# An attention and two-layer expert kernel on one core: side steps and the products with v placed from a table of slots

## The chip, the cores and the metric

The kernel runs on one core of a Trainium2 chip. TensorE (PE) multiplies matrices, VectorE (DVE) and ScalarE (ACT) work on elements, GpSimd (POOL) does further elementwise work, and SyncE (SP) issues the transfers. Every engine follows its own list of instructions in a fixed order and waits on semaphores for the others. The metric is device time in microseconds (us) of one execution. The kernel before takes 518.95 us, the median of three runs (518.83 to 519.52).

## The reference

Three layers follow each other. Only the first is touched by the change.

```python
q_assign = argmax(q_n . c_n)            # nearest of 16 centroids, per query; k_assign likewise, per key
mask   = q_assign[..., :, None] == k_assign[..., None, :]
scores = where(mask, (q @ k.T) / 8, -1e9)
x = softmax(scores) @ v                 # 2 batches x 8 heads, 768 tokens, 64 wide
x = moe(x)                              # x @ w_in, a rational function P(h) / Q(h), @ w_out
out = moe2(x)                           # soft routing by phi to 8 experts with w1, w2
```

All of it is float32. The weights `w_in` and `w_out` reach the chip as 64-bit numbers and have to be turned into float32 on it ("decoding").

## The kernel before, in words

**Units and slots.** Attention handles two heads at a time: 8 pairs, p = 0 to 7. A pair has 12 units, each 128 queries of one head by all 768 keys, so there are 96 units. The main loop runs over n, and one turn of it is called a slot (slot n in what follows). In slot n, TensorE first turns the 128 x 768 softmax weights of unit n (six transpositions, line 359, tile sT). Then it computes the scores of unit n + 2 (four products, lines 335 and 336, tile s). VectorE takes the scores of unit n + 2 out of PSUM, scaled and with their row minimum (line 344, e). ScalarE takes the exponential of unit n + 1 (line 348) and copies the turned weights of unit n (line 365, eT). There is one PSUM tile for s and one for sT, so the scores of the next unit cannot start until VectorE has read the last ones, and the next transpositions wait for ScalarE's copy.

**Products with v.** Six units (one half of a pair) form a group g, and six blocks of products with v belong to it (line 372, av, one block is two heads). The string AV says how many blocks TensorE does in each slot; they come after the scores.

**Side steps.** Three kinds of work are laid between these. (1) `prep(p)` makes the operands of a pair two pairs ahead: scores against the centroids (line 216), their scaled copy and transposition, the one-hot cluster of each token (`best`, `first`: lines 231 to 246), its transposition and mask (`ohT`, `masks`), and the split of k and q into two rounded parts on GpSimd (`ksplit`, `qsplit`); transfers (`ksplit(1)`, `ksplit(2)`, `qspreads`, `mspread`: 4 + 2 + 6 + 8 per pair) then spread these into the operand tiles k1, k2, q1, q2. (2) `norm(g)` and `a2_x(g)` divide by the softmax sum and split the result. (3) 32 decoding steps, one every 2.65 slots (list DEC): a load, two bit operations, an exponent on ScalarE, mantissa and sign on VectorE (lines 492, 493, 499, 503), a product on GpSimd (line 508), a store; for `w_out` also a product with phi (`tr`, `tcopy`, `mm`, `keep_`, every fourth time `fin`, `total`).

**What sets the order.** The order on every engine is written by this loop. A dictionary `plan` holds, for each slot and each kind of phase, the side steps of that slot in the order in which they were added. VectorE's steps of slot n stand before its line 344 for unit n + 2; GpSimd's and SyncE's are issued at the slot's head; TensorE's transpositions (phase P) stand between scores and products with v, its other products (phase T) behind them. Before, a step's slot follows from offsets in the return lists of `prep`, `norm`, `wphi_steps` (and PREP1 for pair 1). SyncE issues in program order and rotates over eight completion semaphores: each transfer waits until the one eight places before it has landed.

After attention the second stage (lines 747 to 780, 48 units) follows, then the last layer.

Of the kernel before, what the change touches and what calls it, by code (L numbers as in the profile page):

```python
# [8 lines left out]
F32 = mybir.dt.float32  # L9
F32R = mybir.dt.float32r  # L10
# [4 lines left out]
ALU = mybir.AluOpType  # L15
# [37 lines left out]
def tile_kernel(ctx, tc, qT, kT, v, cenT, cenP, consts, constsb, ab, w_in, w_out, phi, w1, w2, out, dbg=None):  # L53
# [59 lines left out]

    LEAD = 2
    PREP1 = (0, 0, 1, 1, 2, 3, 3, 4, 5, 6, 2, 3, 5, 7)
# [23 lines left out]
    def first_pair(r, o, f):  # L139
# [51 lines left out]
        def back(nxt):  # L191
# [3 lines left out]
        rest = [(0, "G", lambda: f["qsplit"](1)),  # L195
                (1, "S", lambda: f["qspreads"](slice(HS, S))),
                (1, "D", lambda: q_rows(0, 1)),
                (2, "D", lambda: q_rows(1, 1))]
        return front, back, rest

    def prep(p):
# [81 lines left out]
        def qsplit(c, done=None):  # L283
# [17 lines left out]
        if p == 0:  # L301
            return first_pair(r, o, locals())
        b = 1 if p == 2 else 0
        return [
            (1 + b, "T", scores),
            (2 + b, "A", scaled),
            (3 + b, "P", scT),
            (4 + b, "D0", lambda: best(0)),
            (4 + b, "D0", lambda: best(1)),
            (5 + b, "D0", lambda: first(0)),  # L310
            (8, "G", lambda: ksplit(0)),
            (6 + b, "D0", lambda: first(1)),
            (7 + b, "D0", lambda: first(2)),
            (7 + b, "P", ohT),
            (8 + b, "A", masks),
            (11, "G", lambda: qsplit(0)),
            (12, "G", lambda: qsplit(1)),
            (9, "S", lambda: ksplit(1)),
            (10, "S", lambda: ksplit(2)),
            (10 + b, "S", mspread),  # L320
            (13, "S", qspreads),
        ]
# [52 lines left out]
    def norm(g):  # L375
# [24 lines left out]
        at = (0, 1, 2, 4, 5) if g < 2 * NP - 1 else (0, 1, 1, 2, 3)  # L400
        return list(zip(at, ("G0", "D0", "G0", "P", "A"), (total, over, wide, rows, keep_)))

    def a2_x(g):
# [21 lines left out]
        return [(0, "D0", scale), (1, "G", split)]  # L425
# [54 lines left out]
    def decode_steps(i, src, dst, after=None):  # L480
# [38 lines left out]
        def store():  # L519
            SP.dma_start(dst, hold["w" if after else "w2"])  # L520

        return [(-4, "L", dma), (0, "D1", bits), (1, "A", expo), (1, "D1", mant), (2, "D1", sign),
                (3, "G0", value)] + ([(4, "S", store)] + after(hold) if after else [(4, "G", parts), (5, "S", store)])
# [4 lines left out]
    def wphi_steps(f):  # L528

        def steps(hold):  # L530
# [26 lines left out]
            def total():  # L557
# [3 lines left out]
            return [(4, "P", tr), (5, "A", tcopy), (6, "T", mm), (7, "D1", keep_)] + \  # L561
                ([(7, "P", fin), (8, "D1", total)] if f % 4 == 3 else [])
# [19 lines left out]
    def w_load(n):  # L582
        for a in range(2):
# [32 lines left out]
    steps = prep(1)  # L616
    early = [steps.pop(0)[2] for _ in range(3)]
# [3 lines left out]
    for slot, (_, eng, fn) in zip(PREP1, steps):  # L621
        plan.setdefault(slot, {}).setdefault(eng, []).append(fn)
    pend = None
    for n in range(-LEAD, NSL + 6):
# [10 lines left out]
        if k == 4 and n > 0 and p + 2 < NP:  # L635
            add(n, prep(p + 2))
# [18 lines left out]
        run(n, ("S", "D0", "D", "D1", "D2", "G0", "G"))  # L655
# [668 lines left out]
```

## Time and profile before

| | before |
|---|---|
| median of 3 runs | 518.95 us (518.83 to 519.52) |
| profiled execution | 518.78 us, its span 517.0 us |
| first and last start of a transposition of attention (line 359) | 20.4 and 271.4 us |
| TensorE busy in the span | 501.1 us (97%) |
| VectorE, ScalarE, GpSimd busy | 404.5, 362.7, 274.3 us |

A busy share of TensorE near 100% does not say that it works at its peak: matmuls are pipelined and their ends are modelled, so a wait can hide inside an instruction that seems to run. What a slot costs is read from the distance between the first transpositions of neighbouring units.

### The profile page before, as it was taken

The numbers are of one execution on the slowest core, as the hardware profiler recorded it, in microseconds if no ns is written. First come the engines' busy times: TensorE is split into PE (matmuls) and PEld (weight loads), VectorE is DVE, ScalarE is ACT, GpSimd is POOL, SyncE is SP. The second block draws the span as 40 slices with busy tenths as digits, with TensorE's granted clock in tenths as the row PEclk, the third lists the DMA queues.
The fourth block names the chain that finished last, engine by engine and source line by source line (L and its number), as shares of the span: only waits on it lengthen the run. The fifth ranks groups of instructions, "written<-read, shape, count | busy, mean of one in ns | idle before, by whom it ended". The sixth has DMA issues, their size and how long they took to land.

```text
span 517.0 us, 9835 instructions
## 1 busy us (share of the span) xinstructions
PE 501.1 (97%) x3446; PEld 336.0 (65%) x3446; DVE 404.5 (78%) x746; ACT 362.7 (70%) x646; POOL 274.3 (53%) x316
## 2 busy tenths in 40 slices
PE   8899999999999999999999999999999999999994
PEld 3556666666666666666666877777777768764362
DVE  5698899798998988988642999999799996985022
ACT  2587778888778888778772888879588786861111
POOL 4253876549686496765423856555365544551000
PEclk9999999999999999999999999999999999999999
DMA  7998989787996869873402767766466765789997
GB/s 218 249 227 223 315 244 301 223 248 218 261 298 173 285 200 287 249 216 129 160 5 61 261 226 263 278 223 234 181 228 235 266 231 178 289 325 403 422 418 307
DMA packets 44944, 126.18 MB, mean 244 GB/s; under 512 B 7136, under 2 KB 9696, under 8 KB 40288
## 3 DMA queue, kind: packets, MB, share of 16 engines
q1 hardware_dynamic: 44752, 125.31, 73.9%
q8 instruction: 27, 0.44, 0.4%
q10 hardware_dynamic: 144, 0.26, 0.1%
q14 instruction: 21, 0.17, 0.1%
HBM read 89.56 MB, written 15.73 MB: 204 GB/s over the span
## 4 chain that ended last, share of the span: by engine, by line
PE 67%; DMA 13%; DVE 9%; ACT 5%; SPq 2%; issue 1%; POOL 1%; ACTq 0%; DVEq 0%
PE h L747 9%; PE av L372 9%; PE sT L359 9%; PE h L750 9%; PE h L748 9%; DMA wt<-w 7%; PE s L335 5%; PE s L336 4%; DVE e L344 4%; PE gt L794 4%; DMA raw<-w_out 3%; ACT e L348 2%; PE l L806 2%; SPq L299 2%; ACT eT L365 2%; DMA w_in<-w 1%
## 5 line engine op out<-in xcount | busy, mean ns | idle before, releaser
L348 ACT ACTIVATE e<-e,nv 128x768 f32<-128x768 f32 x96 | 90.0, 937 | 46.7 <-DVE e L344 42.4
L344 DVE TENSOR_SCALAR_CACHE_REDUCE e<-s 128x768 f32<-128x768 f32 x96 | 91.5, 954 | 32.9 <-PE s L336 25.6
L359 PEld LDWEIGHTS sT<-cst,e 128*128 128x128 f32 x576 | 61.3, 140 | 46.6 <-ACT eT L365 24.5
L359 PE MATMUL sT<-cst,e 128*128 128x128 f32 x576 | 83.7, 281 | 2.5 <-ACT eT L365 2.0
L747 PE MATMUL h<-xh,w 128*128 128x512 f32 x192 | 80.6, 420 | 0.0
L365 ACT COPY eT<-sT 128x768 f32<-128x768 f32 x96 | 75.4, 785 | 6.0 <-PE sT L359 5.6
L372 PE MATMUL av<-eT,vt 128*64 128x384 f32 x384 | 77.2, 504 | 0.0
L764 POOL TENSOR_SCALAR q<-u,babs 128x512 f32<-128x512 f32 x47 | 36.3, 771 | 73.9 <-ACT u L762 73.9
L508 POOL TENSOR_TENSOR w<-mh,ex 128x516 f32<-128x516 f32 x32 | 41.2, 1287 | 64.5 <-DVE ex L503 44.9
L748 PE MATMUL h<-xl,w 128*128 128x512 f32 x192 | 75.3, 392 | 0.0
L335 PE MATMUL s<-k,q 128*128 128x384 f32 x192 | 73.5, 383 | 1.7 <-DVE e L344 1.5
L336 PE MATMUL s<-k,q 80*128 80x384 f32 x192 | 65.1, 339 | 1.1 <-DMA k<-kb 0.6
L766 POOL TENSOR_TENSOR q<-q,u 128x512 f32<-128x512 f32 x47 | 60.9, 1297 | 3.8
L750 PE MATMUL h<-xh,w 128*128 128x512 f32 x192 | 52.9, 396 | 0.0
L762 ACT ACTIVATE u<-h 128x512 f32<-128x512 f32 x47 | 27.9, 594 | 27.6 <-PE h L750 24.0
L747 PEld LDWEIGHTS h<-xh,w 128*128 128x128 f32 x192 | 36.1, 188 | 16.2 <-DVE r L780 4.2
L765 DVE TENSOR_TENSOR p<-p,h 128x512 f32<-128x512 f32 x47 | 32.1, 682 | 15.0 <-ACT p L763 14.9
L750 PEld LDWEIGHTS h<-xh,w 128*128 128x128 f32 x192 | 36.0, 188 | 8.6
L335 PEld LDWEIGHTS s<-k,q 128*128 128x128 f32 x192 | 36.4, 189 | 6.7 <-DVE e L344 5.9
L748 PEld LDWEIGHTS h<-xl,w 128*128 128x128 f32 x192 | 36.2, 189 | 6.7 <-issue 0.5
L772 ACT ACTIVATE r<-q,epsc 128x512 f32<-128x512 f32 x47 | 32.8, 698 | 9.2 <-POOL q L766 7.4
L336 PEld LDWEIGHTS s<-k,q 80*128 80x128 f32 x192 | 36.6, 190 | 1.8 <-issue 1.1
(198 smaller groups left out, 930.2 us busy)
## 6 DMA issues: line engine op xcount, KB each, us to landing
wt<-w SPq DMA_DIRECT2D x32, 1024.0 KB, 7.1
w<-w_in SPq DMA_DIRECT2D x96, 256.0 KB, 3.2
raw<-w_in SPq DMA_DIRECT2D x16, 512.0 KB, 5.0
raw<-w_out SPq DMA_DIRECT2D x16, 512.0 KB, 5.7
w_in<-w SPq DMA_DIRECT2D x16, 512.0 KB, 4.9
k<-ka SPq DMA_DIRECT2D x32, 192.0 KB, 5.1
q<-qh SPq DMA_DIRECT2D x28, 192.0 KB, 5.3
w_out<-w SPq DMA_DIRECT2D x16, 256.0 KB, 4.7
```

Of the source, the lines that this page charges most:

```text
L335: PE.matmul(ps[:, c, 0:HS], o["q1"][:, it], o["k1"][:, w], start=True, stop=False)
L336: PE.matmul(ps[:, c, 0:HS], o["q2"][0:80, it], o["k2"][0:80, w], start=False, stop=True)
L344: DVE.tensor_scalar(e, s1s.pop(u)[:, :, 0:HS], -(D ** -0.5), None, ALU.mult, ALU.min, accum_out=nvs[g][:, rest:rest + 1])
L348: ACT.activation(es[u], es[u], AF.Exp, scale=-1.0, bias=nvs[g][:, rest:rest + 1], accum_out=sums[g][:, rest:rest + 1])
L359: PE.transpose(ps[:, j // 3, j % 3 * 128:(j % 3 + 1) * 128], e[:, j, :], ident)
L365: ACT.copy(dst, eTp.pop(u)[:, :, 0:HS].rearrange("p c (j t) -> p c j t", j=3))
L372: PE.matmul(av[g][64 * h:64 * h + 64, 0:HS], vs[g // 2][:, h, j, :], eTs[g][:, h, j, :], start=(j == 0), stop=(j == 5))
L508: POOL.tensor_tensor(w.rearrange("p (r n) -> p r n", r=3), hold["mh"].bitcast(F32), hold["ex"].bitcast(F32), ALU.mult)
L747: PE.matmul(h, wh[:, c, :], xh[t][:, c, :], start=(c == 0), stop=False)
L748: PE.matmul(h, wh[:, c, :], xl[t][:, c, :], start=False, stop=False)
L750: PE.matmul(h, wl[:, c, :], xh[t][:, c, :], start=False, stop=(c == NCC - 1))
L766: POOL.tensor_tensor(q, q, u, ALU.mult)
```

## The change

The offsets and PREP1 go. A table SLOT gives the slot of every side step by number: for the steps of a pair one entry per pair (indexed from the end), for those of a group one per group, for phi one per decoded block. The steps of decoding itself keep their slots. `best`, `first`, `ksplit` and `qsplit` are cut so that each single instruction has a slot of its own. Inside a slot, each engine's steps are sorted by a fixed list (RANK) instead of by the order in which they were added. AV is another string.

```diff
-    PREP1 = (0, 0, 1, 1, 2, 3, 3, 4, 5, 6, 2, 3, 5, 7)
+    SLOT = {
...
+        "best0": (0, 10, 21, 34, 43, 53, 71),
+        "best1": (0, 11, 22, 35, 45, 53, 71),
...
+        "mspread": (5, 18, 30, 43, 54, 64, 79),
...
+        "kspread1": (5, 16, 31, 39, 49, 62, 77),
+        "qspread": (3, 14, 29, 37, 55, 65, 78),
...
+    }
+    RANK = {n: i for i, n in enumerate(
+        "x over best0 best1 f0 f1 f2 keep total mant sign bits".split()
+        + "sum wide ka kb0 kb1 qh0 ql0 qh1 ql1 value parts split".split()
+        + "scaled r tcopy expo masks".split() + "rows scT ohT tr fin".split() + "mm scores".split())}
...
+    def step(slot, name, fn):
+        return slot, (PHASE[name], RANK.get(name, 0)), fn
...
+        def round_k():
+            tile_(t_p, "ka", [128, S], F32R)
+            tile_(t_p, "kb", [128, S], F32R)
+            POOL.tensor_scalar(hold["ka"], r["k"], 1.0, 1.0, ALU.mult, ALU.mult)
+
+        def low_k(c):
+            w = slice(c * HS, (c + 1) * HS)
+            POOL.tensor_tensor(hold["kb"][:, w], r["k"][:, w], hold["ka"][:, w].bitcast(F32), ALU.subtract)
...
-            (4 + b, "D0", lambda: best(0)),
-            (4 + b, "D0", lambda: best(1)),
-            (5 + b, "D0", lambda: first(0)),
-            (8, "G", lambda: ksplit(0)),
...
+        early = [] if p > 1 else EARLY
+        return [steps[n] for n in early], [step(SLOT[n][p - NP], n, fn) for n, fn in steps.items() if n not in early]
...
-        at = (0, 1, 2, 4, 5) if g < 2 * NP - 1 else (0, 1, 1, 2, 3)
-        return list(zip(at, ("G0", "D0", "G0", "P", "A"), (total, over, wide, rows, keep_)))
+        return [step(6 * g + 6, "sum", total)] + [step(SLOT[n][g], n, fn) for n, fn in
+                                                  zip(("over", "wide", "rows", "r"), (over, wide, rows, keep_))]
...
-          "201111111201102021120201102201"
-          "111102111021121101012201112101"
-          "020211120201301101112101101112"]
+          "110211210201101130131010112101"
+          "201012021021120102102210221010"
+          "102030211020301110211011111030"]
...
-            for fn in plan.get(slot, {}).pop(eng, []):
+            for _, _, fn in sorted(plan.get(slot, {}).pop(eng, []), key=lambda x: x[:2]):
                 fn()
...
-        if k == 4 and n > 0 and p + 2 < NP:
-            add(n, prep(p + 2))
+        if k == (2 if p else 4) and n > 0 and p + 2 < NP:
+            add(0, prep(p + 2)[1])
...
-        run(n, ("S", "D0", "D", "D1", "D2", "G0", "G"))
+        run(n, ("S", "D", "G"))
```

**VectorE, slots 69 and 70.** Each piece begins with line 344 for unit 70 and ends with that for unit 72 (its line is 391 in the changed file). L242 and L244 are two steps of `first`, L550 and L558 `keep_` and `total` of phi, L499 the mantissa, L503 the sign, L492 and L493 the bit operations. Before:

```order
L344 TENSOR_SCALAR e,nv<-s_2628 128x768
L242 TENSOR_TENSOR eq<-eq,cb 128x384
L550 COPY wph<-mf 128x128
L499 SCALAR_TENSOR_TENSOR mh<-raw_141,mh 128x3x172
L344 TENSOR_SCALAR e,nv<-s_2658 128x768
L244 TENSOR_REDUCE mr<-eq 128x24
L558 TENSOR_REDUCE wphi_79<-mf 128x128
L503 SCALAR_TENSOR_TENSOR ex<-raw_141,ex 128x3x172
L492 TENSOR_SCALAR ex<-raw_142 128x3x172
L493 TENSOR_SCALAR mh<-raw_142 128x3x172
L344 TENSOR_SCALAR e,nv<-s_2691 128x768
```

Now:

```order
L391 TENSOR_SCALAR e,nv<-s_2621 128x768
L546 SCALAR_TENSOR_TENSOR mh<-raw_141,mh 128x3x172
L391 TENSOR_SCALAR e,nv<-s_2650 128x768
L550 SCALAR_TENSOR_TENSOR ex<-raw_141,ex 128x3x172
L539 TENSOR_SCALAR ex<-raw_142 128x3x172
L540 TENSOR_SCALAR mh<-raw_142 128x3x172
L391 TENSOR_SCALAR e,nv<-s_2683 128x768
```

Two steps of `first`, `keep_` and `total` have left these two slots; the decoding steps have stayed.

**SyncE, the operands of pair 1.** The names in k_1 and q_1 are the second set of operand tiles; the number behind is the head. w_in_138 is the store of the first decoded block (512 KB). Before, the last transfers ahead of pair 1's first unit are:

```order
L264 DMA k_1_1_132<-nh 16x384
L520 DMA w_in_138<-w_502 128x1024
L299 DMA q_1_0_125<-qh 64x768
L299 DMA q_1_0_125<-ql 64x768
L299 DMA q_1_0_126<-qh 64x768
L299 DMA q_1_1_129<-qh 64x768
L299 DMA q_1_1_129<-ql 64x768
L299 DMA q_1_1_130<-qh 64x768
L486 DMA raw_141<-w_in 128x1024
```

Now:

```order
L311 DMA k_1_1_132<-nh 16x384
L332 DMA k_1_0_127<-ka 64x768 x2
L332 DMA k_1_1_131<-ka 64x768 x2
L335 DMA k_1_0_128<-kb 64x768
L335 DMA k_1_1_132<-kb 64x768
L567 DMA w_in_138<-w_515 128x1024
L533 DMA raw_141<-w_in 128x1024
```

The six q transfers have moved ahead of the masks, the six k transfers (two rows stand for two each) are the last, and the store comes behind them instead of in front.

**SyncE, the operands of pair 7.** Masks are the transfers out of nh; each pair has eight. raw loads a block to decode, w_in_138 and w_out_139 are stores of decoded ones. Before, the last transfers of pair 7 were the q parts, with the masks ahead of them and three transfers of decoding between:

```order
L264 DMA q_1_1_130<-nh 16x384
L264 DMA k_1_1_132<-nh 16x384
L520 DMA w_in_138<-w_2825 128x1024
L486 DMA raw_140<-w_in 128x1024
L520 DMA w_out_139<-w 128x512
L299 DMA q_1_0_125<-qh 64x768
L299 DMA q_1_0_125<-ql 64x768
L299 DMA q_1_0_126<-qh 64x768
L299 DMA q_1_1_129<-qh 64x768
L299 DMA q_1_1_129<-ql 64x768
L299 DMA q_1_1_130<-qh 64x768
```

Now the masks are the last, directly behind the q parts, of which the last three stand first here:

```order
L359 DMA q_1_1_129<-qh 64x768
L359 DMA q_1_1_129<-ql 64x768
L359 DMA q_1_1_130<-qh 64x768
L311 DMA q_1_0_126<-nh 16x384
L311 DMA k_1_0_128<-nh 16x384
L311 DMA q_1_0_126<-nh 16x384
L311 DMA k_1_0_128<-nh 16x384
L311 DMA q_1_1_130<-nh 16x384
L311 DMA k_1_1_132<-nh 16x384
L311 DMA q_1_1_130<-nh 16x384
L311 DMA k_1_1_132<-nh 16x384
L533 DMA raw_141<-w_out 128x1024
```

The masks have moved behind the q parts, and the three transfers of decoding that stood between have moved ahead of the whole batch of 20 transfers of the pair.

## Rows read from the trace of the kernel before

**Rows 1.** The page: the span; an engine, busy us (share), instructions.
```profile
span 517.0 us, 9835 instructions
...
PE 501.1 (97%) x3446; PEld 336.0 (65%) x3446; DVE 404.5 (78%) x746; ACT 362.7 (70%) x646; POOL 274.3 (53%) x316
```

**Rows 2.** Stages: start:end, us, engines' busy us (instructions), clock, DMA share, GB/s.
```profile
20.40:34.50 14.10, 13.26 (x77) 8.53 (x78) 13.31 (x25) 11.37 (x21) 3.61 (x5) 1.00 1.05 260
34.50:68.81 34.31, 32.99 (x221) 20.67 (x221) 30.07 (x54) 26.52 (x47) 24.12 (x26) 1.00 0.84 239
68.81:148.92 80.11, 79.02 (x550) 52.84 (x546) 71.44 (x138) 65.85 (x118) 54.47 (x66) 1.00 0.87 260
148.92:244.57 95.65, 94.56 (x639) 62.85 (x635) 84.06 (x156) 77.77 (x139) 65.24 (x76) 1.00 0.76 227
244.57:270.82 26.25, 26.06 (x178) 17.30 (x176) 15.04 (x35) 20.96 (x38) 9.20 (x15) 1.00 0.24 81
```

**Rows 3.** TensorE's timeline, units 60 to 64: start us, length us, instruction.
```profile
181.19 0.87 PE L359 MATMUL sT<-cst,e 128*128 128x128 f32 x6
...
183.49 0.87 PE L359 MATMUL sT<-cst,e 128*128 128x128 f32 x6
...
186.24 0.87 PE L359 MATMUL sT<-cst,e 128*128 128x128 f32 x6
...
189.18 0.87 PE L359 MATMUL sT<-cst,e 128*128 128x128 f32 x6
...
191.84 0.88 PE L359 MATMUL sT<-cst,e 128*128 128x128 f32 x6
```

**Rows 4.** VectorE's groups, 18:270 us: count, busy us, mean ns, idle before.
```profile
L344 DVE TENSOR_SCALAR_CACHE_REDUCE e<-s 128x768 f32<-128x768 f32 x96 | 91.5, 954 | 32.9 <-PE s L336 25.6 <-ACT e L348 4.0 <-ACT eT L365 2.6
L499 DVE SCALAR_TENSOR_TENSOR mh<-raw,mh 128x516 f32<-128x516 uint32 x32 | 31.6, 989 | 0.0
L503 DVE SCALAR_TENSOR_TENSOR ex<-raw,ex 128x516 int32<-128x516 int32 x32 | 28.3, 885 | 2.2 <-ACT ex L496 2.1
...
L492 DVE TENSOR_SCALAR ex<-raw 128x516 int32<-128x516 int32 x32 | 21.7, 677 | 0.0
```

**Rows 5.** Line 499 alone: count, shortest/median/longest ns, first and last start.
```profile
L499 DVE SCALAR_TENSOR_TENSOR mh<-raw,mh x32: 678/800/1777, 27.9 to 247.8; 128x516 f32<-128x516 uint32 x32
```

**Rows 6.** The timeline round slots 71 and 72, VectorE and TensorE.
```profile
211.89 1.50 DVE L499 SCALAR_TENSOR_TENSOR mh<-raw,mh 128x516 f32<-128x516 uint32 x1
...
213.11 0.87 PE L359 MATMUL sT<-cst,e 128*128 128x128 f32 x6
213.30 0.95 DVE L344 TENSOR_SCALAR_CACHE_REDUCE e<-s 128x768 f32<-128x768 f32 x1
...
214.31 0.44 PE L335 MATMUL s<-k,q 128*128 128x384 f32 x1 [0.33 <-DVE e L344]
```

**Rows 7.** TensorE in slot 10, the scores of unit 12.
```profile
46.80 0.41 PE L335 MATMUL s<-k,q 128*128 128x384 f32 x1 [0.29 <-DVE e L344]
47.70 0.42 PE L336 MATMUL s<-k,q 80*128 80x384 f32 x1 [0.48 <-DMA q<-ql]
```

**Rows 8.** SyncE's timeline: start us, length us, issues.
```profile
40.25 0.53 SPq L520 DMA_DIRECT2D w_in<-w  x1
...
55.23 2.85 SPq L278 DMA_DIRECT2D k<-ka  x4
```

**Rows 9.** DMA issues, 18 to 245 us: count, KB each, median us to landing.
```profile
q<-qh SPq DMA_DIRECT2D x28, 192.0 KB, 5.3
```

**Rows 10.** The same for 96 to 104.5 us.
```profile
q<-qh SPq DMA_DIRECT2D x4, 192.0 KB, 7.8
```

**Rows 11.** The timeline where attention ends, TensorE and ScalarE.
```profile
270.82 0.87 PE L359 MATMUL sT<-cst,e 128*128 128x128 f32 x6 [0.17 <-ACT eT L365]
...
271.73 0.80 ACT L365 COPY eT<-sT 128x768 f32<-128x768 f32 x1 [0.96 <-PE sT L359]
...
273.07 0.50 PE L747 MATMUL h<-xh,w 128*128 128x512 f32 x1
```

More of the change, by code (lines that the diff above doesn't have):

```diff
@@ L112, in tile_kernel @@
     NBUF = 2
+    SLOT = {
+        "xs": (15, 20, 25, 33, 41, 44, 49, 55, 65, 68, 73, 81, 84, 94, 96, 100),
+        "scores": (5, 16, 27, 39, 50, 67),
+        "scaled": (6, 17, 30, 41, 51, 68),
+        "scT": (9, 19, 31, 42, 52, 69),
[5 rows of a table added]
+        "ohT": (1, 16, 24, 40, 50, 59, 77),
+        "masks": (4, 17, 27, 41, 51, 62, 78),
+        "mspread": (5, 18, 30, 43, 54, 64, 79),
[9 rows of a table added]
+        "qspread": (3, 14, 29, 37, 55, 65, 78),
+        "over": (8, 15, 19, 25, 34, 37, 43, 52, 55, 62, 67, 73, 79, 86, 91, 98),
+        "wide": (8, 15, 20, 27, 34, 37, 43, 52, 55, 63, 68, 73, 79, 86, 93, 98),
+        "rows": (8, 16, 20, 27, 34, 37, 45, 52, 55, 63, 69, 75, 79, 87, 93, 98),
+        "r": (9, 17, 22, 28, 35, 39, 46, 53, 56, 64, 70, 76, 81, 89, 94, 99),
+        "tr": (8, 14, 19, 23, 29, 37, 42, 45, 52, 59, 63, 65, 71, 77, 83, 87),
+        "tcopy": (9, 15, 22, 25, 31, 39, 44, 49, 55, 62, 64, 68, 72, 80, 86, 91),
+        "mm": (14, 18, 23, 29, 35, 40, 48, 50, 58, 63, 65, 71, 79, 83, 88, 92),
+        "k0": (16, 19, 26, 31, 38, 44, 49, 52, 61, 65, 68, 73, 82, 85, 90, 93),
+        "fin": (34, 55, 75, 95),
+        "tot": (37, 56, 77, 96),
+    }
[3 more added lines that the diff above has]
+        + "scaled r tcopy expo masks".split() + "rows scT ohT tr fin".split() + "mm scores".split())}
+    PHASE = {n: e for e, ns in dict(
+        D="x over best0 best1 f0 f1 f2 keep total mant sign bits q_rows",
+        G="sum wide ka kb0 kb1 qh0 ql0 qh1 ql1 value parts split", A="scaled r tcopy expo masks",
+        P="rows scT ohT tr fin", T="mm scores", S="store kspread0 kspread1 mspread qspread", L="load").items()
+        for n in ns.split()}
+    def step(slot, name, fn):
+        return slot, (PHASE[name], RANK.get(name, 0)), fn
     LEAD = 2
-    PREP1 = (0, 0, 1, 1, 2, 3, 3, 4, 5, 6, 2, 3, 5, 7)
+    EARLY = ("scores", "scaled", "scT")
     OPENW = 4
@@ L193, in back @@
             idle(3)
[L195 to L198, printed above, removed]
+        rest = [step(0, "qh1", lambda: f["qsplit"](1)),
+                step(1, "qspread", lambda: f["qspreads"](slice(HS, S))),
+                step(1, "q_rows", lambda: q_rows(0, 1)),
+                step(2, "q_rows", lambda: q_rows(1, 1))]
         return front, back, rest
@@ L423, in split @@
                 done += n
-        return [(0, "D0", scale), (1, "G", split)]
+        return [step(6 * g + 12 if g < 2 * NP - 1 else NSL + 4, "x", scale), step(SLOT["xs"][g], "split", split)]
     NH = H // 2
@@ L520, in store, with at @@
             SP.dma_start(dst, hold["w" if after else "w2"])
-        return [(-4, "L", dma), (0, "D1", bits), (1, "A", expo), (1, "D1", mant), (2, "D1", sign),
-                (3, "G0", value)] + ([(4, "S", store)] + after(hold) if after else [(4, "G", parts), (5, "S", store)])
+        def at(i):
+            steps = [step(max(i - 4, -LEAD), "load", dma), step(i, "bits", bits), step(i + 1, "expo", expo),
+                     step(i + 1, "mant", mant), step(i + 2, "sign", sign), step(i + 3, "value", value)]
+            if after:
+                return steps + [step(i + 4, "store", store)] + after(hold)
+            return steps + [step(i + 4, "parts", parts), step(i + 5, "store", store)]
+        return at
     wph = {}
@@ L615, in tile_kernel @@
     SP.dma_start(coef, ab)
-    steps = prep(1)
-    early = [steps.pop(0)[2] for _ in range(3)]
+    early, steps = prep(1)
     front(early)
@@ L620, in tile_kernel @@
     add(-LEAD + 1, rest)
-    for slot, (_, eng, fn) in zip(PREP1, steps):
-        plan.setdefault(slot, {}).setdefault(eng, []).append(fn)
+    add(0, steps)
     pend = None
```

58 lines of the change are left out of this document (25 added, 33 removed), and 11 rows, old and new, of the table SLOT.

## The prediction

> **What bounds the kernel now.** I read the page first. TensorE is busy for 97% of the 517.0 us, ScalarE and VectorE for far less [rows 1], so the kernel looks bound by TensorE alone, and a change that only moves other work could then give nothing. The page's busy time is no proof of that, so the second view is the table of stages. Its bounds are the first transpositions of units 0, 6, 18, 48, 84 and 95 [rows 2]. Attention fills 250.4 of the 517.0 us, and up to unit 84 VectorE is busy 88 to 94% of each stage [rows 2]. Two engines are nearly full there, and in a slot in which VectorE has more to do than TensorE, TensorE has to wait.
>
> The third view is TensorE's timeline, for the price of a slot. In slots 60 to 63 the first transpositions stand at 181.19, 183.49, 186.24, 189.18 and 191.84 [rows 3]. Slot 60 holds one block with v: 2.30 us. Slot 61 has four transpositions for phi besides: 2.75. Slot 62 holds two blocks: 2.95. Slot 63 has one block and the product with phi: 2.66. So a second block costs 0.65, turning for phi 0.45, its product 0.36. Priced in this way from slots without a wait, TensorE's own list is 13.1 us for slots 0 to 5, 31.7 for 6 to 17, 77.5 for 18 to 47 and 91.6 for 48 to 83, together 213.9. The stages took 14.1, 34.3, 80.1 and 95.65 [rows 2], together 224.2. TensorE loses 10.3 us there: 1.0, 2.6, 2.6 and 4.05.
>
> Where it loses them is seen round slot 72. The transpositions of unit 72 start at 213.11, and the scores should follow 0.61 later, at 213.72. They start at 214.31, released by VectorE's line 344, which only started at 213.30 behind a mantissa step [rows 6]. That is 0.59 us in one slot. One other loss is of another kind: in slot 10 the second score product starts at 47.70, 0.90 behind the first, and waits for the transfer of q [rows 7]; undisturbed it follows after 0.26 (an estimate from the neighbouring pairs of products), so 0.64 us are lost to the transfer. The other 9.6 us I put down to VectorE.
>
> **VectorE's list.** Priced by mean durations [rows 4] less the 0.08 or so by which an instruction's record overlaps the next (the mantissa at 211.89 ends at 213.39, the next starts at 213.30 [rows 6]): line 344 with its wait 0.97, mantissa 0.91, sign 0.80, each bit operation 0.60, the smaller steps between 0.10 and 0.62. Take slot 70. Before, VectorE has 0.97 + 0.47 (`first`) + 0.59 (`total`) + 0.80 + 1.20 = 4.03 us, and TensorE 2.30 + 0.34 = 2.64 (one block and the transpositions of `rows`). Excess: 1.39. Now VectorE has 0.97 + 0.80 + 1.20 = 2.97, and TensorE three blocks, 3.60. Excess: none. Summed in this way over slots 0 to 83, VectorE's list is longer than TensorE's in 34 slots before, by 2.0, 3.6, 4.4 and 6.9 us in the four stages, 17.0 in all. The losses to VectorE, without the 0.64, are 1.0, 2.0, 2.6 and 4.05. The ratio is 0.50, 0.55, 0.59 and 0.59: about 0.57 of an excess turns into time, and the rest is taken up by the slack of a slot or so between the engines. That the ratio holds in four stages is the best evidence that this is the mechanism.
>
> **The change part by part.**
> The work is the same: the same instructions of the same shapes on every engine, none added, none taken away. What changes is what stands beside what.
> - TensorE's list over slots 0 to 83 becomes 213.0 (14.0, 30.2, 76.7 and 92.1): a few switches between kinds of products less. Term: -0.9 us.
> - VectorE's excess falls to 9.6 us in 23 slots (2.0, 0.8, 3.8 and 2.9). At the ratios of the stages the loss is 1.0 + 0.4 + 2.2 + 1.7 = 5.3 instead of 9.6. Term: -4.3. Bounds: if the ratio fell to 0.4 on what is left, the loss would be 3.8 and the term -5.8; if VectorE's excess did not matter at all, the term is 0.
> - Pair 1's operands. Before, the store of the first decoded block was issued at 40.25 [rows 8], in front of the six q transfers; now it stands behind the last transfer that unit 12 needs. It moves 512 KB, at the 239 GB/s of that stage [rows 2] 2.2 us. The wait of 0.64 should go. Term: -0.6 (bounds 0 and -0.64); next late there is VectorE, which is in the second term already.
> - The end. Slots 84 to 94 cost TensorE 25.7 us by its list before and 26.5 now: +0.8. Then from the last transpositions (270.82) to the first product of the next stage (273.07) it was 2.25 us, with two blocks of the group before as filler [rows 11]. Now only the transposition of phi stands there, until 1.1 us after the transpositions began, and the last six blocks wait for ScalarE's copy, which ends 271.73 + 0.80 - 270.82 = 1.71 after it [rows 11]: TensorE stands idle for 0.6, but what comes before those blocks is 0.5 us shorter. Term: +0.8 - 0.5 = +0.3. Behind this the order of the stages is the same, and TensorE has work throughout.
> - GpSimd's split is cut into single pieces. It has idle time enough (busy 68 to 70% of the stages from unit 6 to 84 [rows 2]), and its steps wait for no slot, so I take 0, for as long as each piece is done before its transfer.
> - SyncE's queue. The last batches of operands now stand three slots ahead of the scores that need them for pairs 3, 4, 5 and 7, where they stood five before. Three slots are 7.9 us (224.17 us over 84 slots, 2.67 each [rows 2]). A batch has up to eight transfers at 0.71 each (four took 2.85 [rows 8]), 5.7 us, and lands 5.3 after issue in the median [rows 9]: 11.0 in all for the last one. But the last one is for the second head, needed one slot later still, and SyncE comes to its rows up to a slot early. So at the median landing it just fits, at the 7.8 of the crowded stretch at 96 us [rows 10] it is 2.5 us late. Bounds per batch: 0 and +2.5; I take 0.25, near the lower end because the row of 28 transfers weighs more than the row of four. Term for four batches: +1.0.
>
> Sum: -0.9 - 4.3 - 0.6 + 0.3 + 1.0 = -4.5 against the profiled execution's 518.78 (its span of 517.0 and 1.8 around it), so 514.3. That execution lies 0.17 below the median of the runs, 518.95; for the median I say 514.4.
>
> A rule that speaks against cutting GpSimd's trains. The row shows mantissa steps of the same shape between 678 and 1777 ns, 800 in the median [rows 5] and 989 in the mean [rows 4], and the one behind which slot 72 was late took 1.50 us [rows 6]. The Trainium skill (SBUF — State Buffer, "Who interferes with whom") says that a VectorE instruction with two SBUF inputs and a GpSimd instruction that reads SBUF share one read interface, and whichever starts first keeps it for its whole length. The spread of the row agrees. By the rule alone, more single pieces are more chances to be caught; by the rows, GpSimd's planned work in the mantissa and sign slots stays about as it was (84 us before, 82 now, by the same kind of list), so my sum keeps the means.
>
> **The rivals.**
> (1) The loss is not VectorE's excess but the handing over from engine to engine, a fixed price per slot. Then only the other terms are left: 518.78 - 0.9 - 0.6 + 0.3 + 1.0 = 518.6. Against it: the loss per slot differs from 0.09 (stage 3) to 0.17 (stages 1 and 2 without the transfer), while the ratio to the excess does not.
> (2) Operands come late; this one ends slower. SyncE's batches are landing-bound, as at 96 us: with 7.8 us instead of 5.3 every one of the four batches costs 2.5 instead of 0.25, together +10.0: 514.3 + 9.0 = 523.3. For it: the transfers' share is 0.84 to 0.87 in two stages [rows 2], and shorter slots press the same bytes into less time. Against it: before, the same transfers stood in the same crowd and only unit 12 waited visibly. It turns the change slower than before when the landing costs more than about 1.4 us a batch, that is from a landing of 6.7 us.
> (3) GpSimd's pieces catch VectorE more often. Pair by pair, three trains become five or six pieces, some 17 more; each may hold a two-input step for half a piece, 0.5 us: 8.5 us of VectorE's time, of which a share of 23 slots in 84 at the ratio 0.57 counts: +1.3, so 515.7.
> (4) What is left of the excess stands behind slots in which TensorE has more, so hardly any turns into time, at a ratio of 0.25: the loss is 2.4, and the time 511.4.
>
> **How the numbers follow.** Forecast 0.60, with its own range 512.3 to 517.0; rival 1 0.15, rival 2 0.13, rival 3 0.06, rival 4 0.06. A measurement of this kernel can tell 0.2%, about 1.0 us, from no change, so faster means below 517.9. Of the forecast all but 0.02 is faster, rivals 3 and 4 are, and a fifth of rival 1: 0.73. Same: most of rival 1 and the edge of the forecast, 0.13. Slower: rival 2 and a rest of rival 1, 0.14. The range: below, it takes in most of rival 4 (511.6); above, it takes in rival 1 and the mild cases of rival 2 (519.5). What lies outside, most of rival 2 and the edges, is some 0.2.
>
> **What would show it.** In the profile after, the same five stages should take about 15.0, 31, 79 and 94 us, and 26.5 for the last; the time from the first to the last transposition should fall by 4 to 6 us, and everything behind it should keep its length. VectorE's idle time at line 344 should still be released by TensorE's scores, and TensorE's idle time before its scores by line 344 should shrink. In slots 34, 46, 58 and 82 the scores should start about 0.6 after the transpositions; if they wait there for transfers, rival 2 holds. If the stage from unit 18 to 84 keeps its 175.8 us although the lists fit better, the mechanism is wrong. If mantissa and sign have longer means than 989 and 885 ns, rival 3 holds.

## The result, and the profile after

The changed kernel is slower: 521.82 us in the median of 20 runs (517.95 to 525.65), against 519.09 of 20 runs of the kernel before (517.62 to 520.77). The ratio is 1.0057 (95% interval 1.0037 to 1.0077). The forecast was 514.4.

The profiled execution took 520.44 us, its span 518.6. The same five stages as in [rows 2], by the same view (start:end, us, each engine's busy us, clock, DMA share, GB/s); units 0, 6, 18, 48, 84 and 95 now begin at these times:

```profile
20.82:37.16 16.34, 13.95 (x85) 8.95 (x86) 15.09 (x26) 11.98 (x22) 9.10 (x10) 1.00 0.95 264
37.16:67.64 30.48, 30.46 (x206) 20.28 (x204) 26.50 (x51) 25.52 (x47) 20.28 (x23) 1.00 0.92 265
67.64:151.64 84.00, 79.22 (x537) 53.49 (x535) 71.22 (x135) 65.61 (x117) 59.09 (x69) 0.98 0.79 234
151.64:246.55 94.91, 92.75 (x655) 62.96 (x653) 82.52 (x159) 78.59 (x140) 62.54 (x72) 1.00 0.76 225
246.55:273.17 26.62, 26.62 (x185) 17.39 (x181) 14.30 (x35) 21.13 (x38) 8.42 (x14) 1.00 0.34 119
```

The forecast was 15.0, 31, 79, 94 and 26.5. Four stages are within 1.4 us of it; the one from unit 18 to 48 is 5.0 over. Its busy columns alone don't say why: all engines have about the work that they had in [rows 2], save GpSimd with 59.1 us (54.5 before, with three instructions fewer between these bounds). Slot by slot (distance of neighbouring first transpositions, less TensorE's list) the stage loses 7.3 us, and 5.6 of them in slots 34 and 35, which take 6.37 and 4.06 us. TensorE's timeline in slot 34:

```profile
115.77 0.55 PE L440 MATMUL mf<-cst,rb 128*128 128x128 f32 x3 [3.86 <-POOL rb L435]
...
116.70 1.48 PE L406 MATMUL sT<-cst,e 128*128 128x128 f32 x6
```

The `rows` transpositions waited 3.86 us for GpSimd's `wide`, and the next transpositions of slot 35 took 1.48 us in place of the 0.87 of [rows 3]. One step back, GpSimd's timeline: its piece kb0 of pair 4 waited for a transfer, and the split (xh, xl) and `wide` (rb) stood behind it.

```profile
111.27 1.54 POOL L320 TENSOR_TENSOR kb<-rawk,ka 128x384 fp32r<-128x384 f32 x1 [3.50 <-DMA k<-kb]
112.78 0.29 POOL L468 TENSOR_SCALAR xh<-x 128x128 fp32r<-128x128 f32 x1
...
115.20 0.51 POOL L435 TENSOR_SCALAR rb<-s 128x384 f32<-128x384 f32 x1
```

And one step further, SyncE's timeline: that transfer is pair 3's kspread1, which still reads the only tile kb. The table has it in slot 31 behind the masks' eight transfers of slot 30.

```profile
100.93 1.49 SPq L311 DMA_DIRECT2D q<-nh  x1
102.47 0.58 SPq L311 DMA_DIRECT2D k<-nh  x1
...
106.26 0.59 SPq L311 DMA_DIRECT2D k<-nh  x1
106.89 1.24 SPq L335 DMA_DIRECT2D k<-kb  x2
```

So the chain is: eight issues of about 0.6 us, a transfer issued at 106.89, a tile free at 111.27, `wide` at 115.20, TensorE at 115.77. Before, kb of pair 4 was written in slot 36, not 33, and its transfer of pair 3 had been issued in slot 26. While SyncE issued the masks' transfers the transfers' share was 0.47, and 0.92 in the 12.6 us behind them (the windows' view again):

```profile
100.93:106.89 5.96, 5.96 (x38) 3.96 (x39) 4.84 (x10) 5.78 (x12) 4.02 (x5) 1.00 0.47 109
106.89:119.50 12.61, 8.75 (x51) 6.30 (x49) 6.99 (x14) 6.73 (x12) 8.70 (x12) 0.88 0.92 260
```

A like chain stands in slot 65 with the other tile: ka of pair 7 waited for pair 6's transfers out of ka, `value` stood behind it, and the transpositions `tr` of the same slot behind that (SyncE, GpSimd, then TensorE). Slot 65 loses 2.1 us. One link differs: kb's two transfers above landed within 3.6 us of their issue; these four took 7.0 to 8.0, and each of their issues had itself waited for the landing of the transfer eight places before.

```profile
186.67 4.34 SPq L332 DMA_DIRECT2D k<-ka  x4
```
```profile
197.16 0.83 POOL L316 TENSOR_SCALAR ka<-rawk 128x768 fp32r<-128x768 f32 x1 [2.37 <-DMA k<-ka]
197.95 1.28 POOL L555 TENSOR_TENSOR w<-mh,ex 128x516 f32<-128x516 f32 x1
```
```profile
199.29 0.66 PE L586 MATMUL mf<-cst,w 128*128 128x128 f32 x4 [1.87 <-POOL w L555]
```

What was forecast to get better did. In slot 10 the scores no longer wait for q [rows 7], and in slot 72 they follow the transpositions after 0.68 us, in place of 1.20 [rows 6]:

```profile
47.78 0.42 PE L382 MATMUL s<-k,q 128*128 128x384 f32 x1
48.04 0.34 PE L383 MATMUL s<-k,q 80*128 80x384 f32 x1
...
216.12 0.88 PE L406 MATMUL sT<-cst,e 128*128 128x128 f32 x6
...
216.80 0.44 PE L382 MATMUL s<-k,q 128*128 128x384 f32 x1
```

### The profile page after: what moved, and what is told of

It reads as the page before. It is cut to its first block, busy times and chain, and to the rows that moved or that the text cites. A ratio compares the mean times of both kernels' runs of the same rounds, so it can differ in the third digit from the quotient of the medians.

```text
span 518.6 us, 9831 instructions
## 1 busy us (share of the span) xinstructions
PE 498.3 (96%) x3446; PEld 338.5 (65%) x3446; DVE 401.4 (77%) x746; ACT 363.0 (70%) x646; POOL 275.2 (53%) x316
## 4 chain that ended last, share of the span: by engine, by line
PE 70%; DMA 11%; DVE 8%; ACT 4%; POOL 2%; issue 2%; SPq 2%; POOLq 0%; DVEq 0%; ACTq 0%
PE av L419 10%; PE sT L406 10%; PE h L798 9%; PE h L801 9%; PE h L799 9%; DMA wt<-w 7%; PE s L382 5%; PE s L383 4%; PE gt L845 4%; DVE e L391 3%; PE l L857 2%; ACT e L395 2%; SPq L311 1%; DMA rawk<-kT 1%; PE dg L919 1%
## 5 line engine op out<-in xcount | busy, mean ns | idle before, releaser
L406 PEld LDWEIGHTS sT<-cst,e 128*128 128x128 f32 x576 | 62.4, 141 | 42.9 <-ACT eT L412 21.7
L419 PEld LDWEIGHTS av<-eT,vt 128*64 128x64 f32 x384 | 23.2, 136 | 26.2 <-issue 24.0
```

The costliest lines, as they stand in the source:

```text
L406: PE.transpose(ps[:, j // 3, j % 3 * 128:(j % 3 + 1) * 128], e[:, j, :], ident)
L419: PE.matmul(av[g][64 * h:64 * h + 64, 0:HS], vs[g // 2][:, h, j, :], eTs[g][:, h, j, :], start=(j == 0), stop=(j == 5))
```

## The experiments

All ratios are to the kernel before on the same chip. Slot times are distances of first transpositions in the profiled execution; "attention" runs from unit 0's to unit 95's. That is one execution of each, and it can lie off the median: e5's took 520.78 us (median 517.90), e8's 523.12 (519.46), e10's 520.79 (518.14).

| kernel | ratio (95% interval) | slot 24 | 34 | 35 | 39 | 65 | 66 | attention |
|---|---|---|---|---|---|---|---|---|
| before | 1 | 2.75 | 2.22 | 2.91 | 2.30 | 3.61 | 1.86 | 250.42 |
| changed | 1.0057 (1.0037, 1.0077) | 3.43 | 6.37 | 4.06 | 2.78 | 4.39 | 2.43 | 252.35 |
| e1_kb0_later | 1.0013 (0.9988, 1.0038) | 2.48 | 2.42 | 2.66 | 5.63 | 5.92 | 3.27 | 252.19 |
| e2_kb_two | 1.0006 (0.9978, 1.0034) | 3.43 | 2.71 | 2.67 | 5.49 | 4.35 | 2.44 | 252.63 |
| e3_ka_later | 1.0017 (0.9997, 1.0038) | 3.44 | 5.95 | 4.17 | 2.80 | 2.31 | 2.30 | 251.85 |
| e4_fill_wait | 1.0033 (1.0009, 1.0057) | 3.43 | 6.06 | 2.60 | 2.29 | 6.67 | 4.17 | 254.79 |
| e5_split_back | 0.9966 (0.9941, 0.9991) | 7.46 | 2.34 | 2.66 | 2.29 | 3.01 | 2.44 | 251.06 |
| e6_split_alone | 1.0052 (1.0026, 1.0078) | 2.75 | 3.17 | 3.43 | 2.30 | 3.34 | 3.33 | 253.31 |
| e7_split_back_late | 0.9975 (0.9948, 1.0002) | 7.63 | 2.33 | 2.66 | 2.29 | 3.02 | 2.45 | 251.06 |
| e8_list_alone | 0.9998 (0.9973, 1.0023) | 2.75 | 2.22 | 2.94 | 2.30 | 3.09 | 1.85 | 251.30 |
| e9_from_pair4_back | 0.9895 (0.9870, 0.9921) | 3.44 | 2.34 | 2.66 | 2.29 | 3.00 | 2.44 | 245.85 |
| e10_kb_spread_early | 0.9988 (0.9962, 1.0013) | 2.48 | 3.74 | 2.60 | 2.62 | 6.45 | 4.13 | 250.84 |
| e11_masks_scalar | 1.0984 (1.0946, 1.1021) | 2.49 | 2.34 | 2.66 | 2.29 | 4.19 | 3.31 | 304.64 |
| e12_back_masks_scalar | 1.0989 (1.0964, 1.1015) | 2.49 | 2.34 | 2.66 | 2.29 | 3.45 | 2.67 | 302.44 |

**Is it the wait for the tile? (e1, e2)**

```diff
-        "kb0": (3, 12, 23, 33, 47, 56, 70),
+        "kb0": (3, 12, 23, 34, 47, 56, 70),
```


> One number of the table is changed: GpSimd's copy kb0 of pair 4 goes from slot 33 to slot 34, where the list puts it behind the group's `wide` (rb) and the split. Theory (the copy waits for the transfer that still reads the single tile kb, and `wide`, then TensorE's `rows`, stand behind it): slot 34 falls from 6.4 to about 2.2 to 2.5 us, slot 35 from 4.06 to about 2.67, so this stage falls from 84.0 to about 78.5 us and the time by about 5 us, to about 0.996 of the kernel before. Rival (`over`, `wide` and `rows` of one group in one slot are too tight by themselves): slot 34 stays within 1 us of 6.4. Second rival (the time is lost to a lower granted clock whatever waits): the wait goes, but the clock stays at about 0.991 and the time gains under 2 us.

```diff
-            hold[tag] = pool.tile(shape, dt, tag=tag, name=tag)
+            more = {"bufs": 2} if tag == "kb" else {}
+            hold[tag] = pool.tile(shape, dt, tag=tag, name=tag, **more)
```


> The tile kb gets a second buffer; the table stays as changed. Theory: the copy of pair 4 in slot 33 no longer waits for the transfer of pair 3, so GpSimd runs it at once, `wide` is done before TensorE asks for it, and slots 34 and 35 take about 2.2 to 2.5 and 2.67 us, as with the copy one slot later; time about 5 us under the changed kernel. Rival (the slot is too tight by itself, or the transfer is not what GpSimd waits for): slot 34 stays near 6.4 us.

Both take the wait out of slot 34, e1 by the order, e2 with the order untouched; with two buffers GpSimd runs kb0 at 107.91 without idle time before it (first fence). So the wait for the tile, and no tight slot, is what held slot 34. Neither gives the 5 us that I expected; by the ratios they are 2.3 and 2.6 us below the changed kernel. Slot 39 now takes 5.6 and 5.5. In e1 TensorE waits there for the raw k of pair 5 (second fence; its load on SyncE is the third):

```profile
107.91 1.00 POOL L321 TENSOR_TENSOR kb<-rawk,ka 128x384 fp32r<-128x384 f32 x1
```
```profile
127.85 0.51 PE L263 MATMUL mf<-rawk,cT 128*32 128x384 f32 x1 [2.52 <-DMA rawk<-kT]
```
```profile
116.40 0.33 SPq L174 DMA_DIRECT2D rawk<-kT  x1
...
127.82 1.14 SPq L335 DMA_DIRECT2D k<-kb  x2
```

That load was issued at 116.40 and took over 11 us behind the crowd (the seven loads of raw k took 5.1 in the median before). My reading, which no run tests alone: the crowd had to be worked off, and without the wait in slot 34 it is met in slot 39.

**The other tile, and the clock (e3, e4)**

```diff
-        "ka": (1, 11, 16, 32, 39, 56, 65),
+        "ka": (1, 11, 16, 32, 39, 56, 66),
```


> One number of the table is changed: GpSimd's copy ka of pair 7 goes from slot 65 to slot 66, so that `value` of slot 65 no longer stands behind it. Theory: the wait of 1.87 us of TensorE's `tr` in slot 65 goes, slot 65 loses its 2.08 us, and the time falls by 1.5 to 2 us against the changed kernel; slots 34 and 35 stay at 6.4 and 4.1. Rival (`value` and `tr` in one slot are too tight by themselves): slot 65 keeps at least 1 us of it, since value alone takes 1.28 us on GpSimd.

Slot 65 falls from 4.39 to 2.31 as expected, but slots 71 and 72 lose 1.2 and 0.8 instead (the scores wait for VectorE's line 391), and the stage from 48 to 84 takes 94.72 in place of 94.91. The ratio falls from 1.0057 to 1.0017, some 2 us as expected, though attention in the profile is only 0.5 us shorter; the two intervals just touch.

```diff
             hold["m"] = m_tile()
+            if g == 4:
+                for _ in range(9):
+                    PE.matmul(hold["m"][:, 0:256], ident, cst[:, 0:256], start=True, stop=True)
```


> Nine FP32 products of 128 by 256 columns, whose result nothing uses, are put ahead of the three `rows` transposes of slot 34, so that TensorE has work in the 3.9 us in which it waits for `wide`; GpSimd's wait is left as it is. Theory (the idle TensorE is what the lower clock of slot 35 follows): slot 34 stays at 6 to 7 us, the granted clock stays at 1.0 and slot 35 takes 2.67 instead of 4.06 us; the time falls by about 1.4 us. Rival (the clock falls for another reason): slot 35 stays at about 4 us.

Slot 34 stays at 6.1 and slot 35 falls to 2.60: the theory holds. The clock rows, of the changed kernel and then of e4:

```profile
116.00:116.50 0.50, 0.50 (x7) 0.50 (x6) 0.00 (x0) 0.00 (x0) 0.50 (x1) 0.95 1.14 262
...
118.50:119.00 0.50, 0.50 (x4) 0.45 (x2) 0.00 (x0) 0.50 (x2) 0.42 (x2) 0.50 1.03 266
...
119.50:120.00 0.50, 0.50 (x4) 0.19 (x4) 0.50 (x1) 0.00 (x0) 0.50 (x2) 0.63 1.13 408
```
```profile
110.00:125.00 15.00, 15.00 (x102) 11.98 (x101) 11.82 (x24) 9.11 (x16) 12.38 (x16) 1.00 1.03 302
```

After 3.86 us without work TensorE ran at 0.50 (1.2 GHz) for about 3.4 us; with filler in the wait it kept 1.00 (2.4 GHz). This wait thus cost 1.4 us more than itself. The ratio falls from 1.0057 to 1.0033, 1.2 us, which the intervals do not tell from nothing; in this profile slot 65 lost 6.7 - 4.4 = 2.3 us more than in the changed kernel's. The lower clock goes with slot 66 of the table too: in e1, e4 and e10 TensorE waited 2.83, 3.47 and 3.25 us in slot 65, about the end of that wait the clock fell to 0.50, for 3.4, 6.8 and 6.8 us, and slot 66 took 3.3 to 4.2 us (2.4 in the changed kernel, whose clock stayed 1.00 there).

**Which part of the change (e5, e6, e7, e8).** In e5 and e7 ten rows of the table go back to the old slots for pairs 2 to 7 (one shown); e6 has only those ten from the table; e8 has none, and old AV, so only the fixed list is new.

```diff
-        "kspread1": (5, 16, 31, 39, 49, 62, 77),
+        "kspread1": (5, 14, 26, 38, 50, 62, 74),
```


> The changed kernel, with one part of it undone for pairs 2 to 7: GpSimd's pieces ka, kb0, kb1, qh0, ql0, qh1, ql1 and the transfers kspread0, kspread1 and qspread stand in the slots that they had before (ka and kb together eight slots behind the start of the pair's steps, their transfers one and two slots later, so that a tile is never written while the pair before still waits for its transfer). All other steps, and the products with v, stay as in the table. The first four runs showed that a wait that is taken away at slot 34 or 65 comes back at slot 39 or 65, while the transfers of slots 33 to 40 stand in one crowd from 109 to 135 us. Theory (the crowd of transfers and the tiles that wait for it cost what the lists gave): slots 34, 35, 39 and 65 lose under 0.6 us each, the stage from unit 18 to 48 takes 78 to 80 us, that from 48 to 84 93 to 95, and the time is 4 to 5 us below the kernel before, a ratio of 0.991 to 0.993. Rival (it is the new slots of `over`, `wide`, `rows`, `value` and `tr`, too tight in themselves): two or more of those slots still lose over 1 us and the ratio stays at 1.000 or above.

> The other half: every step and every product with v stands in the slot that it had before, save GpSimd's pieces of the split and the transfers kspread and qspread, which stand in the slots of the table. Theory: the waits on the crowded transfers appear here too, at or near slots 34 to 40 and 65, and the time is 3 to 6 us above the kernel before, a ratio of 1.006 to 1.012. Rival (the new slots of the other steps are what is too tight): ratio 0.999 to 1.002, no slot that loses over 1.3 us save slot 10 as before.

> As e5_split_back, and `first` of pair 1 spread over three slots (f1 in slot 2, f2 and the transpositions ohT in slot 3, where the table puts all three in slot 1). Theory: the 1.2 us that TensorE waits in slot 1 for VectorE's comparison go, and the rest is as in e5: about 1 us below e5, a ratio of 0.989 to 0.992. Rival: what waits for the masks of pair 1 comes as late in slots 5 to 10, so that stages 1 and 2 together keep their sum of e5.

> Only the last part of the change: every step and every product with v stands in the slot that it had before, and inside a slot each engine follows the fixed list. By their order the lists of TensorE, VectorE and ScalarE are then those of the kernel before; on GpSimd `value` and the parts of decoding stand behind ka, kb or q pieces that share their slot, in place of ahead of them, and the transfers of kb stand behind those of the masks. Theory: nothing that TensorE waits for moves past its time, ratio 0.999 to 1.001. Rival (`value` behind up to 3.7 us of pieces delays the transpositions `tr` one slot later): ratio 1.002 to 1.006, with TensorE waiting at `tr` in the slots of four pairs.

The list alone is worth nothing (0.9998). The split's new slots alone cost 0.52%, nearly as much as the whole change (0.57%) but less than the 0.6 to 1.2% expected; without them the rest gains 0.34%. In e6 the chain of slot 65 is there in slot 66, where the old table has `tr` (SyncE, GpSimd, TensorE). Slots 34 and 35 take 0.95 and 0.5 us more than before, but by the profile TensorE waits there for VectorE and ScalarE.

```profile
191.65 2.83 SPq L332 DMA_DIRECT2D k<-ka  x4
```
```profile
199.20 0.95 POOL L316 TENSOR_SCALAR ka<-rawk 128x768 fp32r<-128x768 f32 x1 [5.24 <-DMA raw<-w_out]
```
```profile
201.44 0.66 PE L586 MATMUL mf<-cst,w 128*128 128x128 f32 x4 [1.26 <-POOL w L555]
```

The row of ka names another transfer as the releaser, but that one landed only at 200.46, after ka had started; the fourth of pair 6's ka transfers landed at 199.12, 0.08 us before it.

e5 gains less than expected; in its profile the mixture of old and new rows makes a new crowd. Slot 24 takes 7.5 us: VectorE's `bits` waits for a decoding load, which SyncE issued at 80.75, behind six transfers of q and the eight of the masks.

```profile
86.10 0.69 DVE L539 TENSOR_SCALAR ex<-raw 128x516 int32<-128x516 int32 x1 [4.03 <-DMA raw<-w_in]
```
```profile
70.47 0.47 SPq L359 DMA_DIRECT2D q<-qh  x1
...
75.09 0.85 SPq L311 DMA_DIRECT2D q<-nh  x1
...
80.75 0.53 SPq L533 DMA_DIRECT2D raw<-w_in  x1
```

e7 takes the wait of slot 1 down from 1.2 to 0.4 us, but attention takes the same 251.06, and the first two stages together 46.7 us (47.1 in e5): its rival holds nearly.

**A version that beats both (e9).** Pairs 4 to 7 of the split go back, pairs 2 and 3 keep the table; pair 1 as in e7.

```diff
-        "kb0": (3, 12, 23, 33, 47, 56, 70),
+        "kb0": (3, 12, 23, 36, 48, 60, 72),
...
-        "kspread1": (5, 16, 31, 39, 49, 62, 77),
+        "kspread1": (5, 16, 31, 38, 50, 62, 74),
```


> A version that should beat both kernels: the table as changed, but GpSimd's pieces of the split and their transfers stand in their old slots for pairs 4 to 7 only (pairs 2 and 3 keep the table), and pair 1 has f1, f2 and ohT in slots 2, 3 and 3. In e5_split_back, where pairs 2 and 3 went back too, 5.0 us were lost in slot 24: a weight load for decoding stood on SyncE behind q's six and the masks' eight transfers, and VectorE's `bits` waited for it. Theory (the order on SyncE and the wait for its transfers, and nothing else, are what the change lost): slot 24 loses about 0.9 as in the changed kernel, slots 34 to 40 under 0.6 each, stage 18 to 48 takes 78 to 79 us, stage 48 to 84 about 94, the ratio is 0.985 to 0.991. Rival (the crowd of transfers is simply full, and any order of it makes some step late by 3 to 5 us): some slot of 18 to 48 loses over 3 us again, and the ratio is 0.995 to 0.999.

514.06 us in the median of 6 runs (512.08 to 515.92), ratio 0.9895, with slot 24 and the stages as its theory had them. The edit moves GpSimd's pieces and their transfers together, so it does not tell the two apart. The five stages, and slot 34 on TensorE, now without a wait:

```profile
20.40:36.02 15.62, 14.42 (x86) 8.87 (x86) 14.10 (x26) 12.03 (x22) 9.45 (x10) 1.00 0.96 262
36.02:67.52 31.50, 31.29 (x205) 20.44 (x203) 27.27 (x51) 25.67 (x47) 20.23 (x23) 1.00 0.88 257
67.52:145.76 78.24, 77.34 (x536) 52.19 (x534) 70.59 (x135) 65.49 (x117) 56.47 (x65) 1.00 0.83 248
145.76:239.65 93.89, 92.88 (x656) 62.88 (x654) 82.71 (x159) 78.88 (x140) 67.55 (x77) 1.00 0.80 241
239.65:266.25 26.60, 26.60 (x185) 17.37 (x181) 14.66 (x35) 21.14 (x38) 8.66 (x14) 1.00 0.27 89
```
```profile
110.28 0.87 PE L406 MATMUL sT<-cst,e 128*128 128x128 f32 x6
...
111.70 0.49 PE L440 MATMUL mf<-cst,rb 128*128 128x128 f32 x3
```

**What stands in front on SyncE (e10, e11, e12)**

```diff
-        "kspread1": (5, 16, 31, 39, 49, 62, 77),
+        "kspread1": (5, 16, 29, 39, 49, 62, 77),
```


> One number of the table: the transfers of pair 3's kb, kspread1, go from slot 31 to slot 29, ahead of the eight transfers of the masks (slot 30) in place of behind them; their data are there since slot 23. GpSimd's list is the one of the changed kernel, with kb0 of pair 4 in slot 33 in front of `wide`. Theory (kb0 waits for this transfer, which stood behind 5 us of the masks' issues on SyncE): GpSimd does not wait in slot 33, slot 34 falls from 6.4 to under 3.2 us; what the crowd of transfers does to slot 39 may take back 0 to 3 us of it, so the ratio is 0.997 to 1.004. Rival (kb0 is too long for its slot, whatever the transfer): slot 34 stays above 5.5 us.

kb0 starts at 109.83 without a wait, so the transfer's place behind the masks is what it waited for. Slot 34 falls to 3.74, less far than expected: `rows` still waits 0.76 us for `wide`, since GpSimd now waits 2.59 us earlier on, at qh, for the q transfers. In this profile slots 65 and 66 take back 3.8 of the 4.1 us won in slots 34 and 35. By the ratio this one number is worth 3.6 us: 0.9988, no longer told from the kernel before.

```profile
107.42 0.51 POOL L342 TENSOR_SCALAR qh<-rawq 128x384 fp32r<-128x384 f32 x1 [2.59 <-DMA q<-qh]
...
109.83 1.48 POOL L320 TENSOR_TENSOR kb<-rawk,ka 128x384 fp32r<-128x384 f32 x1
```
```profile
114.28 0.55 PE L440 MATMUL mf<-cst,rb 128*128 128x128 f32 x3 [0.76 <-POOL rb L435]
```

```diff
-                        SP.dma_start(o[h][n][64:80, w].bitcast(F32), nh[at:at + 16, :].bitcast(F32))
+                        ACT.dma_start(o[h][n][64:80, w].bitcast(F32), nh[at:at + 16, :].bitcast(F32))
```


> The changed kernel with one thing altered: the eight small transfers of the masks of each pair (24 KB each) are issued by ScalarE's queue in place of SyncE's. On SyncE they took 0.63 us each in the profile after, 5 us a pair, in which it issued nothing else. Theory (what stands behind them on SyncE was late by that): kspread1 of pair 3 is issued about 4 us earlier, at 102 to 103 us in place of 106.9, and GpSimd's kb0 hardly waits: slot 34 loses under 1.5 us in place of 4.2. The time depends on what ScalarE pays for eight issues: if as much as SyncE, 5 us in every 32 of a pair, which its idle time only just holds, the ratio lies between 0.995 and 1.010. Rival (it is the bytes in the queue, not the issuing): slot 34 still loses 3 to 5 us.

> As e9_from_pair4_back, with the masks' transfers issued by ScalarE's queue. Theory: there little stood behind them, so nothing is won on SyncE (at most 1 us round slots 23 and 24), and what ScalarE pays shows by itself: if it pays as much as SyncE, exp and the copies come late in the slots of the masks, some 1 to 3 us for each of seven pairs, ratio 0.992 to 1.025; if issuing is nearly free for it, 0.987 to 0.990.

Slots 34 and 35 lose nothing in e11, but at a pace so slow that this proves little: the times are 571.76 and 571.62 us. Both price ranges were far off. Round the masks of pair 3 in e11, ScalarE's timeline and then TensorE's:

```profile
122.04 0.51 ACTq L311 DMA_DIRECT2D q<-nh  x1
...
124.79 1.02 ACTq L311 DMA_DIRECT2D k<-nh  x1
127.37 0.51 ACTq L311 DMA_DIRECT2D q<-nh  x1
...
129.87 0.51 ACTq L311 DMA_DIRECT2D k<-nh  x1
130.43 0.94 ACT L395 ACTIVATE e<-e,nv 128x768 f32<-128x768 f32 x1 [6.65 <-DMA q<-nh]
```
```profile
132.19 1.54 PE L406 MATMUL sT<-cst,e 128*128 128x128 f32 x6 [6.45 <-ACT eT L412]
```

The next exponential waits until the last of the eight issues is done, and TensorE behind it: some 7 us in each of seven pairs. Issuing is only part of it. The eight issues last 8.3 us, of which their own records are 5.5; the fifth started at 127.37, when the first had landed (127.35), for ScalarE and SyncE now share the eight completion semaphores, and an issue on ScalarE waits for landings too. And TensorE was granted 0.50 for 3.4 to 10.2 us round each of the seven stops (0.949 in the mean of this execution, 0.991 in the changed kernel's), so the runs do not price an issue alone.

## Why the prediction was wrong

- The step that failed is the one on GpSimd: "its steps wait for no slot, so I take 0, for as long as each piece is done before its transfer". I asked whether a piece is done before its own transfer, not whether the tile that it writes is free of the transfer of the pair before, nor what is queued behind a piece that waits. Both tiles have one buffer. The term I took as 0: slots 34, 35 and 65 lose 5.6 and 2.1 us by it in the profile. Putting pairs 4 to 7 back, pieces and transfers together, gives (84.00 + 94.91) - (78.24 + 93.89) = 6.8 us there; by the ratios, with pair 1's edit, which won nothing in e7, (1.0057 - 0.9895) x 519 = 8.4.
- SyncE's late batches were priced at +1.0 for scores that would wait in slots 34, 46, 58 and 82. In none of these slots did the scores wait for a transfer. The lateness was real, but it was paid at the tile (slots 34, 65) and, with that taken away, at other transfers (slot 39). Rival 2 thus had the sign and a crowd of transfers, at the wrong place. In slot 65 it had the landing too: 7.0 to 8.0 us, where it took 7.8.
- The rest of the sum came out as a total. For slots 0 to 83 it gave 213.0 + 5.3 + 1.0 = 219.3; the changed kernel takes 246.55 - 20.82 = 225.73, without the 7.7 us of slots 34, 35 and 65 218.0. e9 takes 239.65 - 20.40 = 219.25, but it is not the kernel that was priced, so that match is in part luck.
- By stage it did not come out. The losses to VectorE's excess were to be 1.0, 0.4, 2.2 and 1.7; the changed kernel, without those three slots, loses 2.3, 0.3, 1.7 and 0.7, and e9 1.6, 1.3, 1.5 and 1.8. In the first stage TensorE waits 0.80 us for `first` of pair 1 in slot 1 and 0.96 for line 391 in slot 5. That less excess loses less is borne out (12.7 - 7.7 = 5.0 in place of 10.3 before), and with it rival 1, a fixed price per slot, falls, and rival 4 with its 2.4. A fixed ratio of the excess is not shown, and no run moves VectorE's steps alone.
- The wait in slot 10 went, as forecast. The last stage took 26.62 for 26.5, 0.37 more than before, where the term had +0.8. What follows attention's last transposition became 0.75 us shorter (518.6 - 273.17 = 245.4, before 517.0 - 270.82 = 246.2), where it had -0.5.
- Rival 3 falls. The Trainium skill (SBUF — State Buffer, "Who interferes with whom") says that a VectorE instruction with two SBUF inputs contends with a GpSimd instruction that reads SBUF; that more pieces would catch it more often is not borne out. The two steps together have 56.1 us now and 59.9 before [rows 4], the sign alone a little more (905 ns for 885):

```profile
L550 DVE SCALAR_TENSOR_TENSOR ex<-raw,ex 128x516 int32<-128x516 int32 x32 | 29.0, 905 | 1.9 <-ACT ex L543 1.4
L546 DVE SCALAR_TENSOR_TENSOR mh<-raw,mh 128x516 f32<-128x516 uint32 x32 | 27.1, 848 | 0.0
```

- Slot 65 varies from 4.4 to 6.7 us between the changed kernel, e1, e2, e4 and e10, whose edits don't touch it. The traces show what it follows: in all five, ka of pair 7 starts within 0.1 us of the landing of the last of pair 6's ka transfers, and that landing comes 1.2 us (changed, e2), 2.2 (e1), 2.6 (e10) and 2.8 us (e4) after the slot's first transposition, in the order of the slot's length (4.4, 4.4, 5.9, 6.5 and 6.7). Open is what made the landings late, and it is not shown alone that the crowd's bytes, rather than SyncE's order, are what slot 39 met in e1 and e2.

## What to carry to other kernels

When a producer is moved earlier, ask of its output tile who read it last: with one buffer, the piece waits for the previous round's transfer, and everything queued behind it on its engine waits too. Read an in-order queue of transfers as an engine with a list of its own: many small issues in a row hold up a large one, and a wait taken away at one place came back in part at the next (e1, e2, e10), until the transfers were spread otherwise (e9). Filling slots to TensorE's list seems to take away the slack that hid such waits: the split's new slots cost 0.52% in the old lists (e6), and with the new ones, by e9 against the changed kernel, 1.6%.

## What the runs showed of the hardware

- An issue of a 24 KB transfer of the masks held SyncE for about 0.6 us (0.58 and 0.59 in slot 30 of the changed kernel); during eight of them the transfers' share was 0.47, and 0.92 behind them.
- The same issues on ScalarE's queue stopped its next activation for 6.65 us. The Trainium skill (DMA: Bandwidth & Descriptors, "Issuing engines are not separate DMA queues") says that issuing from several engines saves only the sequencer's time for it, which is usually small beside the transfer. The trace of e11 agrees: an issue took 0.60 us in the median, and 3.6 from issue to landing. But on an engine with work of its own the issue, and the wait in front of it, stand in that engine's list: e11 took 9.8% longer.
- In e1 the load issued at 116.40 landed at 127.80, and the eighth issue behind it started at 127.82. In none of the traces did an issue start before the transfer eight places before had landed, and in e1 26 of 397 started within 0.06 us of it. That is the program's rotation over eight completion semaphores; no run shows a limit of the chip.
- TensorE's clock fell to 0.50 0.7 us after it had work again in slot 35 of the changed kernel, and stayed there for 3.4 us. In e10 it fell in slot 65 while TensorE still waited, 1.2 us before its work, and stayed for 6.8.
